# The value products of the last two token groups as seven block products on 2x2 blocks, with a new order of the whole kernel

## The chip, the cores and the metric

The kernel runs on one core of one Trainium2 chip. The time is the device time of one launch in microseconds (us); of several runs the median is taken. A core has five engines that work side by side, each through its own queue in order: PE (TensorE, matrix products, with results in the eight banks of PSUM), DVE (VectorE), ACT (ScalarE), POOL (GpSimd) and SP (SyncE, which here issues DMAs). In the profile PEld is the load of a matmul's weights, which overlaps PE.

## The reference

What is computed is an attention over 4 batches x 8 heads x 768 positions x 64, with three full causal heads and five that see only four first keys and a window of 64, and behind it a feed-forward block with a gate. The attention's output becomes x, 3072 tokens x 512:

```python
def _moe_ref(x, w_gate, w_val, w_out) -> np.ndarray:
    g = x @ w_gate
    silu = g * (1.0 / (1.0 + np.exp(-g)))
    val = x @ w_val
    return (silu * val @ w_out).astype(np.float32)
```

w_gate and w_val are 512 x 1536, w_out is 1536 x 512. Inputs and output are float32; the kernel multiplies in float16 and sums in float32.

## The kernel before

The 3072 tokens are 24 tiles of 128, in six groups (g = 0 to 5) of four tiles, 512 tokens. Attention makes one tile of x after another: transposed q and k, scores (sc), exponentials on ACT (ex), masks (mask), products with v (val), division by the sums (nm), and a transpose into xt, by PE for the first eight tiles and by DMA (xdma) behind them.

For each group and each of 12 blocks j of 128 columns of the 1536, the feed-forward block runs five tasks. gate (L755, matmul at L759) multiplies the four 128-row parts of w_gate with xt: four matmuls of 512 columns into one bank. tanh (L765) on ACT, stt1 (L769) on DVE: (tanh + 1) times the gate's bank, into the buffer sil. vals is the same function as gate with w_val, four matmuls of 512 columns into another bank. stt2 (L775) on DVE: 0.5 x sil x vals' bank, into h_sb in float16.

The product of h with w_out is already made in 2x2 blocks with seven block products (seventh, L860; out<g>.p1 to p7, each 12 matmuls of 256 columns), with weight sums ws (L412), sums of h called hs (hsum, L831, 768 columns of float16, on DVE or POOL), and gathers oe (L886 to L898, mostly on DVE). Group 5 ends with last_sevens. Stores are issued by SP and ACT.

Every piece of work is a task of a plan with dependencies, buffers that it takes, and the engines that may run it. Nothing is scheduled by the compiler: three strings, made beforehand by a planner, fix everything. ORDER has two characters for each task, its number in base 62 (numbers from 3700 up are warming matmuls), and gives the order in which all tasks are written out; each engine runs its own tasks in that order. WAYS has a digit for each task, the engine among the allowed ones. SLOTS has the buffer of each ring that a task takes: raw (11 buffers of 128x1024 f32), sil, sig, xt and others, and for "gv", "o" and "big" a bank of PSUM.

Read out in this way, the old order has, behind the last attention product val23.0, 19 gates, 22 vals and the rest of the out products on PE; 45 stt, 22 oe and 16 hs on DVE; and 7 hs on POOL.

Of the kernel before, what the change touches and what calls it, by code (L numbers as in the profile page):

```python
# [40 lines left out]
WAYS = (
    "000000000000000000000000000000000000000000000000000000000000222212202202222022110100101101110001"
    "212100001000000000000000210012022201011011000000000000001100222212001010000000000001000000000000"
    "001200002201000000000001000000001000000010000000000220120000000000010000002000000000000020000220"
    "000000100100000000200010000000000020000000000000000000000000210002120000000000100000210001001000"
    "002202020020000001001000000002000000000000000021002000000000000000010001000202220000000001000000"
    "000010010000010002212100000010010000000100000000000000000000000000000000000000000000000000000000"
    "000000000000000000000000000000000000000000001100001100000000000000000000000000000000000000000000"
    "000000000000000000000000000000000000000110000000000000000000000000000000000000000000000000000000"
    "000000000000000000010001100011000000000001000000000000000000000000000000000000000000000000000000"  # L50
    "000000001000000000000000000000110000000000000000000000000000000000000000000000000000000000000011"
    "010000110000000000010000000000000000000000000000000000000000000000000000000000000000101000000000"
    "00011001011000000"
)
SLOTS = (
    "001423105578362145403027124360570705626241030877537806901020040702261213013460614010320001264002"
    "430101642120400017524426503000204102434011162426123000254004600122630164212045422322214400101000"
    "130234502420041024003014523602204224610042412422404222212503602112240050221240143404020044225200"
    "005411611104105112030140001212061231013100700167007612020117123450061751067110011241201016300460"
    "216005211560201025311267261606003611020071110012121267117601100231114700730027201774112050100016"  # L60
    "610661265014600771040126102070067023342264511137001010641241015202110066116102500050001512722100"
    "4111232013411120253127611561005111201141005015610026745406"
)
DIGITS = "0123456789ABCDEFGHIJKLMNOPQRSTUVWXYZabcdefghijklmnopqrstuvwxyz"

# [54 lines left out]
def kernel(  # L120
# [13 lines left out]
    nc = tc.nc  # L134
# [11 lines left out]
    DFF = moe_w_gate.shape[1]  # L146
# [57 lines left out]
    def copy(task, dst, src):  # L204
        if task.way == "ACT":
            nc.scalar.copy(out=dst, in_=src)  # L206
        else:
            ENG[task.way].tensor_copy(out=dst, in_=src)  # L208
# [165 lines left out]
    T_w = {}  # L374
# [380 lines left out]
    def gate(g, j, c, wsb, d):  # L755
        xt = xts[g]
        ps = d[g, j, c] = buf("gv", [128, 512], FP, "gv")[:, 0:c[1] - c[0]]
        for kk in range(4):
            nc.tensor.matmul(  # L759
                ps, wsb[:, kk, j * 128:(j + 1) * 128], xt[:, kk, c[0]:c[1]],  # L760
                start=(kk == 0), stop=(kk == 3))

    def tanh(g, j, c):
        sg[g, j, c] = buf("sig", [128, 512], FP, "sig")[:, 0:c[1] - c[0]]
        nc.scalar.activation(out=sg[g, j, c], in_=gs[g, j, c], func=AF.Tanh, scale=0.5)  # L765

    def stt1(g, j, c):
        sl[g, j, c] = buf("sil", [128, 512], FP, "sil")[:, 0:c[1] - c[0]]
        nc.vector.scalar_tensor_tensor(  # L769
            out=sl[g, j, c], in0=sg.pop((g, j, c)), scalar=1.0, op0=ALU.add,  # L770
            in1=gs.pop((g, j, c)), op1=ALU.mult)
# [186 lines left out]
    def tasks_of_sevens(g, T_h):  # L958
# [66 lines left out]
        for x, parts in enumerate(([c11, c12], [c21, c22])):  # L1025
            st = T_st[g, x] = P.add(f"st{g}.h{x}", ["SP", "ACT"],
                                    (lambda x=x: store_half(g, x)), deps=parts)
            T_stored[g, x] = [P.lands(st)]

    for g in range(NG):  # L1030
        w = SIZES[g] * 128
        xs = [T_xe[t] for t in range(FIRST[g], FIRST[g + 1])]
        T_h = {}
        for j in range(NJ):
            parts = [(0, 256), (256, 512)] if g == 0 and j < HALVES else [(0, w)]
            for c in parts:
                a = P.add(f"gate{g}.{j}.{c[0]}", ["PE"],
                          (lambda g=g, j=j, c=c: gate(g, j, c, wg_sb, gs)),
                          deps=xs[c[0] // 128:c[1] // 128] + [T_w["g", j // 2][j % 2]],
                          takes=["gv"])  # L1040
                th = P.add(f"tanh{g}.{j}.{c[0]}", ["ACT"],
                           (lambda g=g, j=j, c=c: tanh(g, j, c)), deps=[a], takes=["sig"])
                s1 = P.add(f"stt1 {g}.{j}.{c[0]}", ["DVE"],
                           (lambda g=g, j=j, c=c: stt1(g, j, c)), deps=[th], takes=["sil"])
# [4 lines left out]
                was = [T_p[g - 2, p] for p in ((6, 7) if j < NK else (3, 4))] if g > 1 else []  # L1049
                was += T_hs[g - 2, 4] if g > 1 and j < NK else []  # L1050
# [3 lines left out]
                P.uses(a, "gv", s1)  # L1054
                P.uses(v_, "gv", s2)
                P.uses(th, "sig", s1)
                P.uses(s1, "sil", s2)
                P.uses(T_first_x[g], "xt", a, v_)
        if g < SEVENS:
            tasks_of_sevens(g, T_h)  # L1060
            continue
# [66 lines left out]
```

## Time and profile before

| | us |
|---|---|
| median of 3 runs (238.83 to 239.19) | 239.04 |
| the profiled execution | 239.03 |
| its span, first to last instruction | 237.2 |
| last matmul's work ends | 233.73 |

| engine | busy us | instructions |
|---|---|---|
| PE | 230.5 | 2211 |
| DVE | 194.5 | 362 |
| ACT | 141.2 | 217 |
| POOL | 110.6 | 132 |

Times in the profile's views count from the span's start. In a view by groups, a row has the line of the program, the engine, the operation, output and input with their shapes, the count, the busy time, the mean duration of one, and the idle time before them with what ended it. A recorded duration of one instruction is longer than the distance at which the next can follow it on the same engine, so distances are read from a timeline, and PE's from the chain of work. Matmuls are pipelined: their recorded durations overlap.

### The profile page before, as it was taken

The page shows a single profiled execution, that of the slowest core. Times are in us where ns is not written, and L with a number is a line of the kernel's source. Part 1 is how long each engine was busy: PE and PEld are TensorE (multiplying, and loading weights), DVE is VectorE, ACT ScalarE, POOL GpSimd, SP SyncE. Part 2 cuts the span into 40 slices and gives each one's busy share as a digit, 9 for nine tenths or more (in the row PEclk, how much of TensorE's full clock was granted, in tenths as well). Part 3 has the DMA queues.
Part 4 walks back from the last instruction along what each step waited for, and adds up shares of the span by engine and source line. Part 5 has one row for each costly group of instructions (what it writes and reads, how often), then busy time and mean ns, then how long its engine had stood idle before and what let it go on. Part 6 is the DMA issues. An engine that isn't in the chain of part 4 may idle for free.

```text
span 237.2 us, 5639 instructions
## 1 busy us (share of the span) xinstructions
PE 230.5 (97%) x2211; PEld 146.0 (62%) x2211; DVE 194.5 (82%) x362; ACT 141.2 (59%) x217; POOL 110.6 (47%) x132
## 2 busy tenths in 40 slices
PE   7899999999999999999999999999999999999994
PEld 2577865655457778655464557766555565557883
DVE  2689999998999699698968989786969867788873
ACT  3699999889599879839575485384242232231010
POOL 7386577937484940998600550884000000525500
PEclk9999999999999999999999999999999999999999
DMA  6999999999999999999798124011620000220044
GB/s 173 351 343 366 326 346 356 358 350 296 271 238 165 236 291 182 289 164 188 196 171 207 34 48 87 4 22 20 203 44 0 3 0 0 87 92 1 20 183 155
DMA packets 67194, 40.73 MB, mean 172 GB/s; under 512 B 25184, under 2 KB 61024, under 8 KB 67168
## 3 DMA queue, kind: packets, MB, share of 16 engines
q1 hardware_dynamic: 65248, 37.50, 63.4%
q10 hardware_dynamic: 1920, 2.88, 3.3%
q8 instruction: 17, 0.28, 0.5%
q14 instruction: 9, 0.07, 0.1%
HBM read 28.31 MB, written 6.29 MB: 146 GB/s over the span
## 4 chain that ended last, share of the span: by engine, by line
PE 92%; DVE 3%; DMA 2%; ACT 1%; issue 0%; DVEq 0%
PE banks L759 51%; PE banks L860 23%; PE banks L567 8%; PE banks L597 6%; PE banks L473 2%; DMA raw<-in_q_dram 2%; PE banks L621 1%; DVE wt_sb L412 1%; DVE sil L769 1%; ACT hq L206 0%; PE banks L321 0%; DVE kT L208 0%; DVE hq L212 0%; DVE qT L208 0%; DVE xb L605 0%; DVE h_sb L775 0%
## 5 line engine op out<-in xcount | busy, mean ns | idle before, releaser
L765 ACT ACTIVATE sig<-banks 128x512 f32<-128x512 f32 (+1 forms) x76 | 42.7, 574 | 54.6 <-PE banks L759 47.5
L759 PE MATMUL banks<-xt,wg_sb 128*128 128x512 f16 (+1 forms) x304 | 71.4, 368 | 0.5 <-DVE sil L769 0.5
L759 PE MATMUL banks<-xt,wv_sb 128*128 128x512 f16 (+1 forms) x304 | 70.9, 368 | 0.0
L579 ACT ACTIVATE e<-banks 128x1024 f16<-128x1024 f32 (+2 forms) x68 | 59.5, 910 | 15.0 <-PE banks L567 6.3
L769 DVE SCALAR_TENSOR_TENSOR sil<-sig,banks 128x512 f32<-128x512 f32 (+1 forms) x76 | 48.8, 655 | 14.3 <-ACT sig L765 13.6
L775 DVE SCALAR_TENSOR_TENSOR h_sb<-sil,banks 128x512 f16<-128x512 f32 (+1 forms) x76 | 48.9, 655 | 2.8 <-PE banks L759 1.8
L860 PEld LDWEIGHTS <-h_sb 128*128 128x128 f16 x420 | 40.4, 98 | 8.5
L759 PEld LDWEIGHTS <-wv_sb 128*128 128x128 f16 x304 | 28.6, 98 | 26.9
L759 PEld LDWEIGHTS <-wg_sb 128*128 128x128 f16 x304 | 28.1, 98 | 27.2 <-issue 0.8
L587 POOL TENSOR_TENSOR e<-e,m 128x640 f16<-128x640 f16 (+1 forms) x17 | 28.0, 1655 | 19.8 <-ACT e L579 19.4
L831 POOL TENSOR_TENSOR h_sb<-h_sb 128x768 f16<-128x768 f16 x13 | 21.2, 1640 | 22.5 <-DVE hs_sb L831 16.7
L898 DVE TENSOR_TENSOR out_sb<-banks,out_sb 128x512 f32<-128x512 f32 x37 | 25.1, 688 | 7.4 <-PE banks L860 7.0
L860 PE MATMUL banks<-wt_sb,h_sb 128*128 128x256 f16 x216 | 26.2, 273 | 0.0
L831 POOL TENSOR_TENSOR hs_sb<-h_sb 128x768 f16<-128x768 f16 x3 | 4.9, 1639 | 45.1 <-PE banks L860 41.2
L860 PE MATMUL banks<-wo_sb,h_sb 128*128 128x256 f16 x204 | 25.1, 273 | 0.0
L597 PEld LDWEIGHTS <-e 128*128 128x128 f16 x472 | 18.0, 97 | 5.8 <-DVE e L587 0.2
L567 PEld LDWEIGHTS <-kT 64*128 64x128 f16 x472 | 14.4, 94 | 9.3 <-issue 8.7
L567 PE MATMUL banks<-qT,kT 64*128 64x128 f16 x472 | 19.7, 218 | 0.2 <-ACT qT L206 0.2
L597 PE MATMUL banks<-vt,e 128*128 128x65 f16 x472 | 19.7, 193 | 0.1
L206 ACT CAST hq<-raw 128x1024 f16<-128x1024 f32 (+1 forms) x16 | 14.7, 936 | 5.2 <-DMA raw<-in_q_dram 3.2
L605 DVE TENSOR_TENSOR xb<-banks,rc 128x512 f16<-128x512 f32 x24 | 16.6, 692 | 0.8
L208 POOL CAST vt<-raw 64x512 f16<-64x512 f32 x23 | 14.0, 607 | 2.3 <-DMA raw<-in_v_dram 1.3
(64 smaller groups left out, 192.9 us busy)
## 6 DMA issues: line engine op xcount, KB each, us to landing
raw<-in_v_dram SPq DMA_DIRECT2D x12, 512.0 KB, 5.8
raw<-in_q_dram SPq DMA_DIRECT2D x8, 512.0 KB, 6.2
raw<-in_k_dram SPq DMA_DIRECT2D x8, 512.0 KB, 5.3
raw<-in_moe_w_gate_dram SPq DMA_DIRECT2D x6, 512.0 KB, 8.6
raw<-in_moe_w_val_dram SPq DMA_DIRECT2D x6, 512.0 KB, 8.2
raw<-in_moe_w_out_dram SPq DMA_DIRECT2D x6, 512.0 KB, 7.9
out_dram<-out_sb SPq DMA_DIRECT2D x6, 512.0 KB, 4.4
raw<-in_q_dram SPq DMA_DIRECT2D x8, 256.0 KB, 6.4
```

Source lines behind the costliest of these rows:

```text
L567: nc.tensor.matmul(sc[:, c:c + n, :], weights, moving, start=first, stop=last)
L579: nc.scalar.activation(out=to, in_=src, func=AF.Exp, scale=scale)
L587: ENG[task().way].tensor_tensor(out=ev, in0=ev, in1=mm, op=ALU.mult)
L597: nc.tensor.matmul(avs[t][:, odd, n * 66:n * 66 + 65], ee, vv, start=(m == 0), stop=(m == len(bl) - 1))
L605: nc.vector.tensor_tensor(out=xb.rearrange("p n o d -> p o n d"), in0=av[:, :, :, 0:64], in1=rc.to_broadcast([128, 2, 4, 64]), op=ALU.mult)
L759: nc.tensor.matmul(ps, wsb[:, kk, j * 128:(j + 1) * 128], xt[:, kk, c[0]:c[1]], start=(kk == 0), stop=(kk == 3))
L765: nc.scalar.activation(out=sg[g, j, c], in_=gs[g, j, c], func=AF.Tanh, scale=0.5)
L769: nc.vector.scalar_tensor_tensor(out=sl[g, j, c], in0=sg.pop((g, j, c)), scalar=1.0, op0=ALU.add, in1=gs.pop((g, j, c)), op1=ALU.mult)
L775: nc.vector.scalar_tensor_tensor(out=hs[g, j][:, c[0]:c[1]], in0=sl.pop((g, j, c)), scalar=0.5, op0=ALU.mult, in1=vs.pop((g, j, c)), op1=A ...
L831: ENG[T_hs[g, x][part].way].tensor_tensor(out=to, in0=a, in1=b, op=op)
L860: nc.tensor.matmul(rooms[g, p][:, x, lo:hi], left[:, j, 128 * x:128 * x + 128], right[:, j, lo:hi], start=(on is None and (j == 0 if apart ...
L898: nc.vector.tensor_tensor(out=cell(*to), in0=room, in1=plus, op=ALU.add)
```

## The change

The vals products of groups 4 and 5 (WINO) are replaced. The group's x is split into 2x2 blocks of 256 columns by token halves x and halves y of the 512 inputs; w_val into blocks of 256 rows by 768 columns. Seven block products take the place of eight. For each s = 0, 1, 2, the tasks wp<g>.<s>.<p> make two 128-column blocks of each half, j = 2s, 2s + 1 and 6 + 2s, 7 + 2s: seven products of four matmuls of 256 columns, where vals had 16 matmuls of 512.

New tasks beside them:

- vw (L412's pattern, function msum): eight differences of parts of w_val, 128x768 float16 in SBUF, made once for both groups, on DVE or POOL.
- xs (xsum): four sums of x blocks for each group, 128x512 float16 in SBUF, on DVE or POOL.
- wy (w_copy): five copies of a bank, 128x512 float32, for each s, on ACT or DVE. P1 is copied from bank X, P6 is then added to bank X by PE and copied, then P7, then P4, so the bank's four products form a chain over PE and the copying engine.
- wa (w_add, c11): a sum of two SBUF pieces, 128x512 float32, on POOL or DVE.
- wb (w_add, c22 and c12): a sum of a bank and an SBUF piece, on DVE.
- stt2 of these groups (stt2_w) reads its second operand from those SBUF pieces (in raw buffers), not from a bank.

The rest of the computation is as before, but ORDER, WAYS and SLOTS are new throughout. Read out, they give:

| | before | after |
|---|---|---|
| vals tasks | 76 | 52 |
| wp tasks | 0 | 42 |
| hs on DVE / POOL | 31 / 17 | 19 / 29 |
| wy on ACT / DVE | | 26 / 4 |
| wa on POOL / DVE | | 4 / 2 |
| wb on DVE | | 12 |
| vw on DVE / POOL | | 3 / 5 |
| xs on DVE / POOL | | 2 / 6 |
| warming tasks beside the first | 2 | 2 |

A stretch of the new order, PE's, DVE's and POOL's tasks, on each line a PE task and what is written between it and the next:

```
PE wp4.2.6    DVE stt2 4.1.0    POOL hs3.2.0
PE wp4.1.7    DVE stt1 4.6.0
PE gate4.7.0  DVE stt1 4.2.0
PE wp4.2.7    POOL hs3.2.1      DVE stt2 4.6.0
PE gate4.9.0  DVE stt1 4.7.0
PE gate4.8.0  DVE stt2 4.7.0
PE wp4.1.4    DVE stt1 4.3.0    POOL xs5.1
PE wp4.2.2    DVE wa4.1.c11
PE wp4.1.5
PE wp5.0.1    POOL xs5.2        DVE wb4.1.c22
PE out3.p6    DVE stt2 4.0.0    POOL wa4.2.c11   DVE oe3.c11
PE wp5.0.2    DVE stt1 4.9.0
PE wp4.1.3    POOL xs5.3        DVE stt2 4.3.0
PE gate5.0.0  DVE oe3.r6
PE wp4.2.4    POOL hs3.4.0      DVE stt2 4.2.0
```

The core of the diff, without the strings:

```diff
+    WINO = {"v": (4, 5), "g": ()}
...
+        ENG[T_mw[mat, i][kk].way].tensor_tensor(
+            out=m_sums[mat, i, kk], in0=a, in1=b, op=ALU.subtract)
...
+        a, b, op = {1: (A[1, 0], A[1, 1], ALU.add), 2: (Z[:, 0], A[0, 0], ALU.subtract),
+                    3: (A[0, 0], A[1, 0], ALU.subtract),
+                    4: (A[0, 1], Z[:, 1], ALU.subtract)}[i]
+        ENG[T_xs[g, i].way].tensor_tensor(out=Z[:, i - 1], in0=a, in1=b, op=op)
+
+    W_ON = {1: "X", 6: "X", 7: "X", 4: "X", 2: "Y", 5: "Z", 3: "Z"}
...
+        for m in range(2):
+            at = slice(128 * (2 * s + m), 128 * (2 * s + m) + 128)
+            for kk in range(2):
...
+                nc.tensor.matmul(
+                    w_rooms[on][:, m], right, left[:, kk],
+                    start=(begins and m == 0 and kk == 0), stop=(kk == 1),
+                    skip_group_check=True)
...
+    def w_copy(mat, g, s, name):
+        to = w_cell(mat, g, s, name)
+        copy(T_wc[mat, g, s, name], to, w_rooms[mat, g, s, "Y" if name == "y2" else "X"])
+
+    def w_add(mat, g, s, name):
+        to = w_cell(mat, g, s, name)
+        other = w_cell(mat, g, s, "y2") if name == "c11" else w_rooms[mat, g, s, "Z"]
+        ENG[T_wc[mat, g, s, name].way].tensor_tensor(out=to, in0=other, in1=to, op=ALU.add)
...
+    def stt2_w(g, j):
+        hs[g, j] = h_sb[:, g % 2, j]
+        nc.vector.scalar_tensor_tensor(
+            out=by_halves(hs[g, j]), in0=by_halves(sl.pop((g, j, (0, 512)))),
+            scalar=0.5, op0=ALU.mult, in1=w_cells("v", g, j), op1=ALU.mult)
...
+            p1 = product(1, xs + w_lo)
+            r1 = copied("r1", [p1])
+            p6 = product(6, [r1, T_xs[g, 2]] + T_mw[mat, 2])
+            u2 = copied("u2", [p6])
+            p7 = product(7, [u2, T_xs[g, 3]] + T_mw[mat, 3])
+            u3 = copied("u3", [p7])
+            p4 = product(4, [u3] + T_mw[mat, 4])
+            p2 = product(2, xs + w_lo)
+            y2 = copied("y2", [p2, r1])
...
+            c11 = added("c11", [y2])
+            c21 = copied("c21", [p4, c11])
...
+            p5 = product(5, [T_xs[g, 1]] + T_mw[mat, 1])
+            c22 = added("c22", [p5, u3])
+            p3 = product(3, [c22, T_xs[g, 4]] + w_hi)
+            c12 = added("c12", [p3])
```

More of the change, by code (lines that the diff above doesn't have):

```diff
@@ new lines @@
+    T_mw = {}
+    for mat in ("v", "g"):
+        for i in range(1, 5) if WINO[mat] else []:
+            T_mw[mat, i] = []
+            for kk in range(2):
+                before = T_mw[mat, i // 2][kk:kk + 1] if i in (2, 4) else []
+                T_mw[mat, i].append(P.add(
+                    f"vw{i}.{kk}" + mat, ["DVE", "POOL"],
+                    (lambda mat=mat, i=i, kk=kk: msum(mat, i, kk)),
+                    deps=[y for n in range(6) for y in T_w[mat, n]] + before,
+                    takes=(["hq"] if i == 4 else ["e"]) if mat == "g"
+                    else [] if kk else ["raw"],
+                    after=T_mw[mat, i][:1]))
@@ new lines, with sums_of_x @@
+    T_xs, T_wp, T_wc = {}, {}, {}
+    def sums_of_x(g, xs):
+        first = T_first_x[g]
+        for i in range(1, 5):
+            T_xs[g, i] = P.add(
+                f"xs{g}.{i}", ["DVE", "POOL"], (lambda i=i: xsum(g, i)),
+                deps=xs + {2: [T_xs.get((g, 1))], 4: [T_xs.get((g, 2))]}.get(i, []),
+                takes=[] if i > 1 else ["raw"], after=[T_xs[g, 1]] if i > 1 else [])
+            P.uses(first, "xt", T_xs[g, i])
+        sum1 = T_xs[g, 1]
+        P.uses(sum1, "raw", T_xs[g, 2], T_xs[g, 4])
@@ new lines, in tasks_of_wino, with product, copied, added @@
+    def tasks_of_wino(mat, g, xs):
+        first, sum1 = T_first_x[g], T_xs[g, 1]
+        for s in range(NK // 2):
+            w_lo, w_hi = list(T_w[mat, s]), list(T_w[mat, s + 3])
+            def product(p, deps, s=s):
+                t = T_wp[mat, g, s, p] = P.add(
+                    f"wp{g}.{s}.{p}" + mat, ["PE"], (lambda: w_product(mat, g, s, p)),
+                    deps=deps, takes=["gv"] if p in (1, 2, 5) else [])
+                if p in (1, 2, 4):
+                    P.uses(first, "xt", t)
+                else:
+                    P.uses(sum1, "raw", t)
+                if p >= 4:
+                    for y in T_mw[mat, {4: 4, 5: 1, 6: 2, 7: 3}[p]]:
+                        if y.takes:
+                            P.uses(y, y.takes[0], t)
+                return t
+            def copied(name, deps, s=s):
+                T_wc[mat, g, s, name] = P.add(
+                    f"wy{g}.{s}.{name}" + mat, ["ACT", "DVE"], (lambda: w_copy(mat, g, s, name)),
+                    deps=deps, takes=["raw"] if name in ("r1", "u2") else [])
+                return T_wc[mat, g, s, name]
+            def added(name, deps, s=s):
+                T_wc[mat, g, s, name] = P.add(
+                    f"w{'a' if name == 'c11' else 'b'}{g}.{s}.{name}" + mat,
+                    ["POOL", "DVE"] if name == "c11" else ["DVE"],
+                    (lambda: w_add(mat, g, s, name)), deps=deps)
+                return T_wc[mat, g, s, name]
+            p1 = product(1, xs + w_lo)
[7 more added lines that the diff above has]
+            y2 = copied("y2", [p2, r1])
+            P.uses(p2, "gv", y2)
+            c11 = added("c11", [y2])
+            c21 = copied("c21", [p4, c11])
+            P.uses(p1, "gv", c21)
+            p5 = product(5, [T_xs[g, 1]] + T_mw[mat, 1])
+            c22 = added("c22", [p5, u3])
+            p3 = product(3, [c22, T_xs[g, 4]] + w_hi)
+            c12 = added("c12", [p3])
+            P.uses(p5, "gv", c12)
@@ L1033 @@
         T_h = {}
+        if g in WINO_ALL:
+            sums_of_x(g, xs)
+        for mat in ("g", "v"):
+            if g in WINO[mat]:
+                tasks_of_wino(mat, g, xs)
         for j in range(NJ):
@@ L1036 @@
             for c in parts:
[L1037 to L1044, printed above, removed]
+                below = ("c11", "c21") if j < NK else ("c12", "c22")
@@ new lines @@
+                head = "r1" if j < NK else "u2"
+                if g in WINO["g"]:
+                    th = P.add(f"tanh{g}.{j}.{c[0]}", ["ACT"], (lambda g=g, j=j: tanh_w(g, j)),
+                               deps=[T_wc["g", g, j % NK // 2, y] for y in below], takes=["sig"])
+                    s1 = P.add(f"stt1 {g}.{j}.{c[0]}", ["DVE"], (lambda g=g, j=j: stt1_w(g, j)),
+                               deps=[th], takes=["sil"])
+                    P.uses(T_wc["g", g, j % NK // 2, head], "raw", s1)
+                else:
+                    a = P.add(f"gate{g}.{j}.{c[0]}", ["PE"],
+                              (lambda g=g, j=j, c=c: gate(g, j, c, wg_sb, gs)),
+                              deps=xs[c[0] // 128:c[1] // 128] + [T_w["g", j // 2][j % 2]],
+                              takes=["gv"])
+                    th = P.add(f"tanh{g}.{j}.{c[0]}", ["ACT"],
+                               (lambda g=g, j=j, c=c: tanh(g, j, c)), deps=[a], takes=["sig"])
+                    s1 = P.add(f"stt1 {g}.{j}.{c[0]}", ["DVE"],
+                               (lambda g=g, j=j, c=c: stt1(g, j, c)), deps=[th], takes=["sil"])
+                    P.uses(a, "gv", s1)
+                    P.uses(T_first_x[g], "xt", a)
@@ new lines @@
+                was = [T_p[g - 2, p] for p in ((6, 7) if j < NK else (3, 4))] if g > 1 else []
+                was += T_hs[g - 2, 4] if g > 1 and j < NK else []
+                P.uses(th, "sig", s1)
+                if g in WINO["v"]:
+                    cells = [T_wc["v", g, j % NK // 2, y] for y in below]
+                    s2 = P.add(f"stt2 {g}.{j}.{c[0]}", ["DVE"],
+                               (lambda g=g, j=j: stt2_w(g, j)), deps=[s1] + cells + was)
+                    T_h.setdefault(j, []).append(s2)
+                    P.uses(s1, "sil", s2)
+                    P.uses(T_wc["v", g, j % NK // 2, head], "raw", s2)
+                    continue
@@ L1053 @@
                 T_h.setdefault(j, []).append(s2)
[L1054 removed]
                 P.uses(v_, "gv", s2)
[L1056 removed]
                 P.uses(s1, "sil", s2)
[L1058 removed]
+                P.uses(T_first_x[g], "xt", v_)
         if g < SEVENS:
```

154 lines of the change are left out of this document (110 added, 44 removed).

## The prediction

> **What bounds the kernel now.** I read the page's busy shares and clock first, then what PE waited for, then a table by stage, then the chain of work that ended last.
>
> ```profile
> PE 230.5 (97%) x2211; PEld 146.0 (62%) x2211; DVE 194.5 (82%) x362; ACT 141.2 (59%) x217; POOL 110.6 (47%) x132
> ...
> PEclk9999999999999999999999999999999999999999
> ```
>
> ```profile
> PE banks L321 <- POOL ident L234: 1.4, 1, 1.4
> PE banks L473 <- DVE hq L212: 0.8, 1, 0.8
> PE banks L759 <- DVE sil L769: 0.5, 1, 0.5
> PE banks L567 <- ACT qT L206: 0.2, 1, 0.2
> ```
>
> ```profile
> core 0: us, PE busy (x) PEld busy (x) DVE busy (x) ACT busy (x) POOL busy (x), PEclk, DMA share, GB/s
> ...
> 170.81:220.62 49.81, 49.81 (x298) 29.01 (x297) 39.56 (x67) 13.29 (x23) 8.07 (x5) 1.00 0.09 30
> 220.62:237.20 16.58, 13.10 (x120) 11.49 (x118) 10.41 (x19) 0.96 (x2) 3.28 (x2) 1.00 0.36 128
> ```
>
> PE is busy 97% of the span at full clock, and over the whole run it waits 2.9 us for named engines. From the end of val23.0 (170.81) to the last gate or value product (220.62) it has no gap: 49.81 of 49.81. So matmul time taken out there is worth its full length, for as long as the other engines keep pace. In that stretch DVE is busy 39.56 of 49.81 us (79%), ACT 27%, POOL 16%. The stage is PE's, and DVE is the next engine in line.
>
> **What PE saves.** Two rows of the chain give the spacing of the two kinds of matmul.
>
> ```profile
> 175.57 5.18 PE banks L759 x24
> 180.75 1.31 PE banks L860 x12
> ```
>
> A 512-column matmul takes 5.18/24 = 0.216 us, a 256-column one 1.31/12 = 0.109. Removed: 2 groups x 12 blocks x 4 = 96 of the first, 20.7 us. Added: 2 groups x 3 values of s x 7 products x 4 = 168 of the second, 18.3 us. PE saves **2.4 us**. Without any new wait: 239.03 - 2.4 = 236.6 (239.03 is the profiled execution; its span is 237.2, and the median of the runs is 239.04, so sums on the one hold for the other).
>
> **What the other engines get.** Durations are in these groups, spacings in the two DVE timelines behind them.
>
> ```profile
> L775 DVE SCALAR_TENSOR_TENSOR h_sb<-sil,banks 128x512 f16<-128x512 f32 x68 | 45.7, 682 | 2.7 <-PE banks L759 1.8
> ...
> L765 ACT ACTIVATE sig<-banks 128x512 f32<-128x512 f32 x68 | 39.8, 596 | 54.6 <-PE banks L759 47.5 <-DVE sil L769 6.8
> ...
> L898 DVE TENSOR_TENSOR out_sb<-banks,out_sb 128x512 f32<-128x512 f32 x37 | 25.1, 688 | 7.4 <-PE banks L860 7.0
> ...
> L831 POOL TENSOR_TENSOR h_sb<-h_sb 128x768 f16<-128x768 f16 x13 | 21.2, 1640 | 22.5 <-DVE hs_sb L831 16.7 <-DVE h_sb L831 5.7
> ...
> L831 DVE TENSOR_TENSOR h_sb<-hs_sb,h_sb 128x768 f16<-128x768 f16 x11 | 6.0, 551 | 0.0
> ...
> L412 POOL TENSOR_TENSOR wt_sb<-wo_sb,wt_sb 128x512 f16<-128x512 f16 x4 | 4.6, 1158 | 6.6 <-DVE wt_sb L412 6.5
> ...
> L206 ACT COPY out_sb<-banks 128x512 f32<-128x512 f32 x3 | 1.7, 582 | 0.0
> ```
>
> ```profile
> 195.78 0.68 DVE L769 SCALAR_TENSOR_TENSOR sil<-sig,banks 128x512 f32<-128x512 f32 x1
> 196.38 0.68 DVE L898 TENSOR_TENSOR out_sb<-banks,out_sb 128x512 f32<-128x512 f32 x1
> ...
> 212.98 0.55 DVE L831 TENSOR_TENSOR h_sb<-hs_sb,h_sb 128x768 f16<-128x768 f16 x1
> 213.45 0.68 DVE L769 SCALAR_TENSOR_TENSOR sil<-sig,banks 128x512 f32<-128x512 f32 x1
> ```
>
> Back to back, a 512-wide f32 instruction costs DVE 0.60 us and a 768-wide f16 sum 0.47. The 30 copies out of banks go 26 to ACT (0.58 each, 15.1 us in a stage where ACT has over 36 us free: hidden) and 4 to DVE. DVE also gets 12 sums wb and two wa (0.60 each), two x sums and three weight differences. Against that, 12 more hs sums move to POOL. In the new order DVE has, from val23.0 to the last stt2: 48 stt (28.8 us), 12 wb (7.2), 9 oe (5.4), two wa (1.2), three wy (1.8), and about 3.1 of nm23, sums and differences: **47.5 us**. PE has there 9 out products of 12 (11.8), 23 gates of 4 x 0.216 (19.9), 37 wp of 4 x 0.109 (16.2) and val23.0 (0.4), 48.2 us, and the last tanh, stt1 and stt2 add about 2.1: 50.3. So DVE goes from 79% to 94%. It still fits, with **2.8 us** to spare, if nothing holds it.
>
> The PSUM chain p1, copy, p6, copy, p7, copy, p4 is covered: the order puts other products between its members. The tightest place is p7 to p3 of group 4, s 0: two gates (1.73 us) against a copy and a sum (0.58 + 0.69). The first p7 also needs vw2.1, xs4.4 and vw3.1 in turn on POOL (1.64 + 1.16 + 1.64), started when val23.1 is due; that ends about 0.5 us after p7's turn. I count this at nothing in the sum, since it overlaps the lateness below, and at up to 1.4 in the range. The new raw buffers come when the loads are over. At the start the order changes little (two fills of the same lengths, the same first products): nothing, plus or minus 0.5 (PE's waits there are 2.4 in all, above). No DMA is added; the stores stay eight on ACT and eight on SP. Behind the last gate stand twelve out products instead of ten. The first that needs a late h, out5.p7, waits for stt2 5.10.0, hs5.1.1 (0.47) and hs5.3.1 on POOL (1.64), with oe4.r6 and r67 ahead in DVE's queue, and comes six products (7.9 us) after the last gate: covered while DVE is on time, and passed on in full once it is late.
>
> **The new hold.** This decides it. stt2 before reads one SBUF operand (sil) and banks. The new stt2 of groups 4 and 5 reads sil and the cells, both in SBUF, and so does wa. Before has no f32 instruction of that kind on DVE; it has f16 ones, and one of them met POOL:
>
> ```profile
> 59.43 1.04 POOL L208 CAST hq<-raw 128x1024 f16<-128x1024 f32 x1 [1.46 <-DMA raw<-in_q_dram]
> ```
>
> ```profile
> 59.53 1.54 DVE L412 TENSOR_TENSOR wt_sb<-wo_sb 128x512 f16<-128x512 f16 x2
> 61.00 0.68 DVE L769 SCALAR_TENSOR_TENSOR sil<-sig,banks 128x512 f32<-128x512 f32 x1
> ```
>
> ```profile
> L412 DVE TENSOR_TENSOR wt_sb<-wo_sb x3: 411/414/1212, 59.5 to 62.8; 128x512 f16<-128x512 f16 x3
> ```
>
> Of three alike, one took 1212 ns against 411 and 414: it started at 59.53 under a POOL cast (59.43 to 60.47) and ended 0.27 us after it. It stood still until POOL was nearly done. With one operand in PSUM there is no such hold:
>
> ```profile
> 204.24 3.24 POOL L831 TENSOR_TENSOR hs_sb<-h_sb 128x768 f16<-128x768 f16 x2 [41.25 <-PE banks L860]
> ```
>
> ```profile
> 204.80 1.28 DVE L775 SCALAR_TENSOR_TENSOR h_sb<-sil,banks 128x512 f16<-128x512 f32 x2
> ```
>
> Two stt2 ran under two POOL sums at 1.28 for both, as elsewhere. [...]
>
> The old order keeps its f16 two-SBUF sums out of POOL's spans. The new order doesn't do so for the new instructions: by the positions of the tasks between PE's, with POOL at 1.64 (768-wide) and 1.16 (512-wide), 9 of the 24 new stt2 start inside a POOL instruction by the latest reading, 20 by the earliest. And POOL's share of the stage rises from 8.07 us in five to about 34 (13 hs, 5 xs, 2 vw, 4 wa).
>
> I walked DVE's order by hand from wp4.2.6, each instruction at 0.60, an stt2 waiting for the POOL instruction under way and the next POOL instruction for it. In us from that point: stt2 4.1.0 0.0 to 0.6, POOL hs3.2.0 0.6 to 2.2, stt1 4.6.0 and 4.2.0 to 1.8, stt2 4.6.0 held to 2.2 and done 2.8, POOL hs3.2.1 2.8 to 4.5, stt1 4.7.0, stt2 4.7.0 held to 4.5; and so on. To stt2 4.10.0, 28 instructions (16.8 us) meet 8 holds (4.6 us); in the rest 8 holds come to 7.2. Together 16 holds, 11.8 us, 0.74 each. As the held row ended 0.27 after POOL where alone it lasts 0.41, I take 0.14 off each: 9.6. Less DVE's 2.8 to spare: **6.8 us late**, and PE waits for it, because gates, p3 and p6 wait for banks, sums and copies that stand behind the held stt2 in DVE's queue.
>
> Bounds of this unknown: nothing, if two f32 operands are not held or DVE always comes first; at the other end 11.8 + 1.4 = 13.2, every hold in full, nothing spare and the first p7 late. The nearest row is the held L412, so I take the hold.
>
> **Sum:** 239.03 - 2.4 + 6.8 = 243.4; say **243.5**.
>
> **Rivals.**
>
> *The hold doesn't come (not slower).* The mechanism: at stt2 of groups 4 and 5, an f32 SCALAR_TENSOR_TENSOR with both operands in SBUF runs beside POOL at 0.60, or gets through first. For it: the only held row is f16, of another operation, and one event. Against it: the same two SBUF operands. Price: DVE at 94% keeps pace, PE loses only the 0.5 at the first p7: 236.6 + 0.5 = 237.1, with 236.3 to 238. It decides where holds sum to under 2.8 (to spare) + 2.4 (PE's gain) = 5.2 us, 0.33 per hold at 16.
>
> *DVE is too full even so.* DVE idled 7.6 us for ACT's tanh in the old stage by the row below; at 94% there is room for 2.8. If half of that idling stays (3.8), it is 1 us late, plus 0.5 to 1.4 at the first p7: 236.6 + 1.0 + 1.0 = 238.6, between 238 and 239.5.
>
> ```profile
> L769 DVE SCALAR_TENSOR_TENSOR sil<-sig,banks 128x512 f32<-128x512 f32 x22 | 14.9, 684 | 7.6 <-ACT sig L765 7.5
> ```
>
> [...]
>
> **How the numbers follow.** Held: 0.60, from 240 to 246.5, point 243.5. Not held: 0.28, 236.3 to 238. Too full: 0.12, 238 to 239.5, of which half lies within 0.2% (0.48 us, about what a measurement of this kernel can tell from no change), a third faster, the rest slower. That gives faster 0.32, same 0.06, slower 0.62. The range takes most of both signs: 236.5 to 246.5; the likeliest case's own is 240 to 246.5.
>
> **What would show it.** Right: the group of stt2 reading sil and raw has a mean over 1.0 us with a minimum near 0.68, its long ones under POOL spans; PE has several us of waits after 171, on DVE; POOL instructions themselves stretch here and there. PE's 256-column products stay at 0.109. Wrong: that group's mean is 0.69, PE's waits stay under 1 us in all, and the end comes 2 us earlier. Wrong on PE's side: 168 matmuls that don't hold 0.109 because their weights change each time, though L860's do the same.

## The result, and the profile after

| | before | after |
|---|---|---|
| median of the runs | 239.0 us (238.83 to 239.19) | 253.23 us (251.71 to 254.62, 4 runs) |
| ratio to before | | 1.0594, 95% interval 1.0511 to 1.0677 |
| profiled execution: time, span | 239.03, 237.2 us | 251.71, 249.9 us |

The change makes the kernel 14.2 us slower. The direction and the mechanism are the predicted ones. The size is not: 4.5 us were forecast, and the result lies above the range. One thing is needed to compare profiles: the first product of group 4 starts at 161.59 us in this one, but up to 3.0 us later in some of those below, mostly because PE waited for DMAs and for ACT (1.5 and 1.0 us in the run with the reduce in group 4 alone, the latest), ahead of all that the edits touch; so beside the medians some stretches are given from that product to the end of the profile.

The page of the changed kernel, busy shares and granted clock:

```profile
PE 231.6 (93%) x2283; PEld 153.4 (61%) x2283; DVE 214.8 (86%) x358; ACT 157.6 (63%) x256; POOL 159.3 (64%) x161
...
PEclk9999999999999999999999999999999899999999
...
L1148 DVE SCALAR_TENSOR_TENSOR h_sb<-sil,raw 128x512 f16<-128x512 f32 x24 | 27.2, 1144 | 0.2
```

PE fell from 97% to 93% of a longer span. DVE is 20.3 us busier (194.5 before) with four instructions fewer. 5.4 of that is the new mix of work: the run whose POOL only writes (below) has the same 358 instructions on DVE and 199.9 us. The other 14.9 are instructions that became longer; the last row is a group of them (busy us, mean ns, idle us before it), taken up below. What PE waited for, late in the kernel (total us, times, longest):

```profile
PE banks L762 <- DVE sil L772: 3.7, 3, 2.5
PE banks L1104 <- DVE raw L1125: 3.4, 2, 2.1
PE banks L1104 <- DVE raw L1084: 1.4, 1, 1.4
```

All three name DVE. Before, the largest wait for DVE anywhere was 0.8. The stage in five slices (busy us and count of PE, PEld, DVE, ACT, POOL, then granted clock, DMA share, GB/s):

```profile
180.00:190.00 10.00, 9.22 (x66) 6.23 (x65) 9.76 (x13) 4.80 (x10) 9.29 (x7) 1.00 0.04 15
190.00:200.00 10.00, 7.92 (x50) 5.33 (x49) 8.17 (x13) 3.67 (x8) 4.34 (x3) 0.83 0.00 0
200.00:210.00 10.00, 8.55 (x62) 5.84 (x61) 9.96 (x14) 2.68 (x6) 5.28 (x3) 1.00 0.01 2
210.00:220.00 10.00, 8.48 (x59) 5.52 (x57) 9.83 (x13) 5.53 (x12) 5.36 (x3) 1.00 0.28 105
220.00:230.00 10.00, 7.46 (x56) 5.21 (x54) 10.00 (x11) 4.25 (x8) 8.97 (x5) 1.00 0.01 2
```

Where PE had no gap before, it now idles 0.8 to 2.5 us of every ten, while DVE is all but full in four of the five. The group that the prediction named, the new stt2 of groups 4 and 5 (minimum, median, maximum ns):

```profile
L1148 DVE SCALAR_TENSOR_TENSOR h_sb<-sil,raw x24: 674/1006/2124, 178.8 to 233.5; 128x512 f16<-128x512 f32 x24
```

The shortest takes 674 ns; the mean is 1144, by the group's row above. DVE's timeline shows which are long, and POOL's shows why (start, duration, us):

```profile
166.17 1.61 DVE L590 TENSOR_TENSOR e<-e,m 128x640 f16<-128x640 f16 x1
167.71 3.42 DVE L1054 TENSOR_TENSOR raw<-wv_sb,raw 128x768 f16<-128x768 f16 x2
...
188.01 1.67 DVE L1148 SCALAR_TENSOR_TENSOR h_sb<-sil,raw 128x512 f16<-128x512 f32 x1
189.61 0.68 DVE L901 TENSOR_TENSOR out_sb<-banks,out_sb 128x512 f32<-128x512 f32 x1
190.21 1.52 DVE L1148 SCALAR_TENSOR_TENSOR h_sb<-sil,raw 128x512 f16<-128x512 f32 x1
...
194.85 0.68 DVE L1148 SCALAR_TENSOR_TENSOR h_sb<-sil,raw 128x512 f16<-128x512 f32 x1
```

```profile
167.40 1.40 POOL L1084 TENSOR_TENSOR raw<-xt,raw 128x512 f16<-128x512 f16 x1
168.76 1.95 POOL L1054 TENSOR_TENSOR raw<-wv_sb 128x768 f16<-128x768 f16 x1
...
187.99 1.15 POOL L1084 TENSOR_TENSOR raw<-xt 128x512 f16<-128x512 f16 x1
189.09 4.14 POOL L834 TENSOR_TENSOR h_sb<-h_sb 128x768 f16<-128x768 f16 x2
193.19 1.16 POOL L1084 TENSOR_TENSOR raw<-xt,raw 128x512 f16<-128x512 f16 x1
```

The stt2 at 188.01 starts 0.02 us after a POOL sum of 1.15 and takes 1.67. The one at 190.21 starts inside the first of two POOL sums and takes 1.52; those two sums take 4.14 together instead of 3.24. Between them the L901 at 189.61, which reads a bank and one SBUF operand, takes its usual 0.68 under the same POOL sum, and the stt2 at 194.85, with POOL idle, takes 0.68. There are holds that the prediction did not count, too: the mask at 166.17 (1.61) and the two weight differences at 167.71 (3.42 for two). In the run whose POOL only writes (below), in the same order, the mask takes 0.48 and the two differences 1.02.

### The profile page after: what moved, and what is told of

It is laid out like the page before. It is cut to its first block, busy times and chain, and to the rows that moved or that the text cites. A ratio compares the mean times of both kernels' runs of the same rounds, so it can differ in the third digit from the quotient of the medians.

```text
span 249.9 us, 5873 instructions
## 1 busy us (share of the span) xinstructions
PE 231.6 (93%) x2283; PEld 153.4 (61%) x2283; DVE 214.8 (86%) x358; ACT 157.6 (63%) x256; POOL 159.3 (64%) x161
## 5 line engine op out<-in xcount | busy, mean ns | idle before, releaser
L762 PE MATMUL banks<-xt,wg_sb 128*128 128x512 f16 (+1 forms) x304 | 73.2, 371 | 4.5 <-DVE sil L772 3.7
L582 ACT ACTIVATE e<-banks 128x1024 f16<-128x1024 f32 (+2 forms) x68 | 59.3, 909 | 12.8 <-PE banks L570 9.8
L762 PE MATMUL banks<-xt,wv_sb 128*128 128x512 f16 (+1 forms) x208 | 47.6, 363 | 0.0
L834 POOL TENSOR_TENSOR h_sb<-h_sb 128x768 f16<-128x768 f16 x18 | 32.2, 1793 | 19.3 <-DVE hs_sb L834 17.4
L590 POOL TENSOR_TENSOR e<-e,m 128x640 f16<-128x640 f16 (+1 forms) x18 | 30.2, 1681 | 11.7 <-ACT e L582 11.3
L778 DVE SCALAR_TENSOR_TENSOR h_sb<-sil,banks 128x512 f16<-128x512 f32 (+1 forms) x52 | 32.7, 642 | 3.6 <-PE banks L762 2.5
L762 PEld LDWEIGHTS <-wv_sb 128*128 128x128 f16 x208 | 19.2, 98 | 17.7
L209 ACT COPY raw<-banks 128x512 f32<-128x512 f32 x27 | 15.2, 590 | 20.5 <-PE banks L1104 9.5
L901 DVE TENSOR_TENSOR out_sb<-banks,out_sb 128x512 f32<-128x512 f32 x37 | 24.8, 684 | 3.5 <-PE banks L863 2.9
L1148 DVE SCALAR_TENSOR_TENSOR h_sb<-sil,raw 128x512 f16<-128x512 f32 x24 | 27.2, 1144 | 0.2
L834 POOL TENSOR_TENSOR h_sb<-hs_sb,h_sb 128x768 f16<-128x768 f16 x6 | 11.5, 1918 | 4.6 <-DVE h_sb L834 4.6
```

What stands on the lines that cost most here:

```text
L582: nc.scalar.activation(out=to, in_=src, func=AF.Exp, scale=scale)
L590: ENG[task().way].tensor_tensor(out=ev, in0=ev, in1=mm, op=ALU.mult)
L762: nc.tensor.matmul(ps, wsb[:, kk, j * 128:(j + 1) * 128], xt[:, kk, c[0]:c[1]], start=(kk == 0), stop=(kk == 3))
L778: nc.vector.scalar_tensor_tensor(out=hs[g, j][:, c[0]:c[1]], in0=sl.pop((g, j, c)), scalar=0.5, op0=ALU.mult, in1=vs.pop((g, j, c)), op1=A ...
L834: ENG[T_hs[g, x][part].way].tensor_tensor(out=to, in0=a, in1=b, op=op)
L901: nc.vector.tensor_tensor(out=cell(*to), in0=room, in1=plus, op=ALU.add)
```

## The experiments

**One operand instead of two.** All 24 new stt2 lose their second SBUF operand. The order, the engines and the instruction's length stay.

```diff
-        nc.vector.scalar_tensor_tensor(
-            out=by_halves(hs[g, j]), in0=by_halves(sl.pop((g, j, (0, 512)))),
-            scalar=0.5, op0=ALU.mult, in1=w_cells("v", g, j), op1=ALU.mult)
+        nc.vector.tensor_reduce(
+            out=by_halves(hs[g, j]), in_=w_cells("v", g, j).unsqueeze(3),
+            axis=mybir.AxisListType.X, op=ALU.max)
```

> The changed kernel with the 24 value instructions of groups 4 and 5 (stt2) replaced by a DVE reduction of the same 128x512 size that reads the cells alone, so the product with sil is left out; same order, same engines, same count. Hold theory: DVE instructions with two SBUF operands stand still under POOL's sums, so with one operand these 24 take 0.68 to 0.70 us each instead of 1.14, POOL's late sums go back to 1.64, and the time falls from 253.2 by the 11 us that they were held and about 2 us of what POOL was held: 239 to 242. Fullness theory: DVE simply has too much work behind group 3; its work is the same here, so 251 to 254.

Measured: 238.89 us, ratio to before 0.9998 (0.997 to 1.0027). That is just under the 239 to 242 of the hold theory. The group, and slices of the stage:

```profile
L1148 DVE TENSOR_REDUCE h_sb<-raw x24: 670/679/686, 178.6 to 220.6; 128x512 f16<-128x512 f32 x24
```

```profile
170.00:180.00 10.00, 8.57 (x61) 5.63 (x60) 8.64 (x16) 4.62 (x8) 5.41 (x4) 1.00 0.25 72
180.00:190.00 10.00, 10.00 (x76) 7.20 (x74) 10.00 (x17) 6.05 (x12) 9.62 (x8) 1.00 0.03 9
190.00:200.00 10.00, 10.00 (x79) 7.64 (x78) 9.68 (x17) 3.53 (x7) 3.73 (x4) 1.00 0.01 2
200.00:210.00 10.00, 10.00 (x69) 6.57 (x68) 9.50 (x17) 6.22 (x12) 7.05 (x5) 1.00 0.28 105
210.00:220.00 10.00, 10.00 (x79) 7.43 (x77) 9.95 (x17) 5.30 (x10) 7.76 (x5) 1.00 0.01 2
```

No instruction of the 24 is held, and from 180 on PE has no gap, with the same instructions on POOL. The second SBUF operand of these 24 is worth 253.23 - 238.89 = 14.3 us by the medians: more than the whole loss. In the profiles, from the first product of group 4 to the end, it is 12.9 (88.3 us in the changed kernel, 75.4 here). The slices show something else, needed below: even without holds DVE has only 0.9 us free in the forty from 180 on, and 1.4 in the ten before.

**POOL writes but does not read.** The stt2 keep both operands, and POOL's late sums become memsets.

```diff
+    def add_up(task, late, out, in0, in1, op):
+        if late and task.way == "POOL":
+            for _ in range(2):
+                nc.gpsimd.memset(out, 0.0)
+            return
+        ENG[task.way].tensor_tensor(out=out, in0=in0, in1=in1, op=op)
...
-        ENG[T_hs[g, x][part].way].tensor_tensor(out=to, in0=a, in1=b, op=op)
+        add_up(T_hs[g, x][part], g >= 3, to, a, b, op)
```

The calls in vw, xs and wa are replaced in the same way.

> The changed kernel with POOL's late sums (hs of groups 3 to 5, weight differences, x sums, wa) replaced by two memsets of the same output each, so POOL reads nothing there and these sums are left out of the result; DVE's work is untouched, with both SBUF operands. Hold theory, if what is held is the reading: stt2 at 0.68 to 0.70 us, time 237 to 240. If POOL holds DVE by writing too: stt2 still near 1.0 us, 246 to 252. Fullness theory: 251 to 254.

Measured: 236.24 us, ratio 0.9898 (0.9851 to 0.9944), just under the 237 to 240 of the hold theory.

```profile
L1154 DVE SCALAR_TENSOR_TENSOR h_sb<-sil,raw x24: 681/685/693, 176.3 to 218.3; 128x512 f16<-128x512 f32 x24
```

The same two-operand instruction is not held by a POOL that only writes, and PE's timeline has no gap from 160 us to its end. 236.2 is close to the 236.6 that the prediction's first sum gave without any new wait: PE's saving is real, and DVE with all its new work keeps pace. (POOL's work is a little lighter here, 147.0 us in all against 154.0 in the first experiment.)

**The late sums on DVE.** Nothing is left out; POOL gets no late sum.

```diff
+        for t in self.tasks:
+            late = t.name[:2] in ("vw", "xs", "wa") or t.name[:3] in ("hs3", "hs4", "hs5")
+            if late and t.way == "POOL":
+                t.way = "DVE"
```

> The changed kernel with the late sums of POOL (hs of groups 3 to 5, weight differences, x sums, wa) moved to DVE at the same places of the order; nothing is left out. Hold theory: stt2 at 0.68 to 0.70 us, but DVE gets about 11 us more work in a stretch that had 2.8 to spare, so about 8 us late: 243 to 248, faster than 253.2 in spite of the added work. Fullness theory: 11 us more work on the engine that bounds: 262 to 266.

Measured: 247.92 us, ratio 1.0363 (1.0339 to 1.0387), at the upper end of the hold theory's 243 to 248.

```profile
180.00:200.00 20.00, 17.51 (x129) 12.43 (x128) 19.62 (x35) 9.12 (x17) 0.00 (x0) 1.00 0.01 4
```

With POOL at rest in the stage the 24 stt2 are not held (a mean of 688 ns), but now DVE is full with work. Taking all late sums off POOL, in this order, is no way out.

**The hold by itself.** Behind the kernel before stand six stages, each of eight DVE instructions, five of them beside a row of POOL instructions; a single execution.

```diff
+    stages = [(lambda: two(fb[:, 0:512]), None, 0),
+              (lambda: two(fb[:, 0:512]), pool_sum, 4),
+              (lambda: two(bank), pool_sum, 4),
+              (lambda: two(fb[:, 0:512]), lambda: nc.gpsimd.memset(pool_out, 0.0), 8),
+              (lambda: two(fb[:, 0:512]),
+               lambda: nc.gpsimd.tensor_copy(out=pool_out, in_=pool_in[0]), 6),
+              (lambda: nc.vector.tensor_reduce(out=half, in_=fa[:, 0:512].unsqueeze(2),
+                                               axis=mybir.AxisListType.X, op=ALU.max),
+               pool_sum, 4)]
```

> The kernel before, and behind its end six stages of eight DVE instructions (128x512 f32 in, f16 out) beside POOL work: both operands in SBUF alone; both in SBUF beside sums 128x768 f16 on POOL; one in SBUF and one in a bank beside these sums; both in SBUF beside memsets; both in SBUF beside copies; a reduction with one SBUF operand beside sums. Hold theory: 0.69 us each in stages 1, 3, 6; in stages 2 and 5 some DVE instructions of 1 to 2.2 us and POOL sums over 1.64; stage 4 at 0.69 if only reading holds. Intrinsic theory (the instruction is slow with two SBUF operands whatever POOL does): 1.1 us in stages 1, 2, 4 and 5 alike.

The stages on DVE (two SBUF operands alone, then beside sums; one operand in a bank beside sums; two beside memsets; two beside POOL copies; a reduce beside sums), and POOL's part in the second and third:

```profile
240.60 5.77 DVE L1114 SCALAR_TENSOR_TENSOR raw<-raw 128x512 f16<-128x512 f32 x8
...
246.67 1.58 DVE L1111 COPY raw<-raw 128x4 f32<-128x4 f32 x1 [0.29 <-POOL raw L1110]
248.16 9.70 DVE L1114 SCALAR_TENSOR_TENSOR raw<-raw 128x512 f16<-128x512 f32 x8
...
259.66 5.73 DVE L1114 SCALAR_TENSOR_TENSOR raw<-raw,banks 128x512 f16<-128x512 f32 x8
...
265.69 0.67 DVE L1111 COPY raw<-raw 128x4 f32<-128x4 f32 x1 [0.30 <-POOL raw L1110]
265.77 5.77 DVE L1114 SCALAR_TENSOR_TENSOR raw<-raw 128x512 f16<-128x512 f32 x8
...
272.74 8.27 DVE L1114 SCALAR_TENSOR_TENSOR raw<-raw 128x512 f16<-128x512 f32 x8
...
282.80 5.72 DVE L1126 TENSOR_REDUCE raw<-raw 128x512 f16<-128x512 f32 x8
```

```profile
246.59 7.82 POOL L1118 TENSOR_TENSOR raw<-raw 128x768 f16<-128x768 f16 x4
...
258.09 6.77 POOL L1118 TENSOR_TENSOR raw<-raw 128x768 f16<-128x768 f16 x4
```

Two of the six rows of eight are longer than the 5.77 alone: 9.70 beside POOL sums, 8.27 beside POOL copies. The hold goes both ways with the sums, since POOL's four take 7.82 there against 6.77 beside the operand in a bank. One operand in a bank, a reduce, or a POOL that only writes: no hold of the eight (5.73, 5.72, 5.77). So of these rows the held ones are those with two SBUF inputs on DVE beside a POOL that reads.

**Half the dose.** The reduce only in group 4:

```diff
+        if g == 4:
+            nc.vector.tensor_reduce(
+                out=by_halves(hs[g, j]), in_=w_cells("v", g, j).unsqueeze(3),
+                axis=mybir.AxisListType.X, op=ALU.max)
+            return
```

> As the first experiment, but only in group 4: its 12 stt2 become a reduce of the cells alone (silu times value left out there), those of group 5 keep their two SBUF operands. Theory (each hold passes on in full): about half of the 14.3 us remains, 244 to 248, and the 12 of group 5 keep a mean over 1.0 us. Rival (one group's holds are what matters, for instance those before the clock's fall at 180 to 200): within 1 us of 238.9 or of 253.2.

Measured: 248.19 us, ratio 1.0376 (1.0358 to 1.0395), just above the 244 to 248 of the hold theory. The groups (busy us, mean ns):

```profile
L1153 DVE SCALAR_TENSOR_TENSOR h_sb<-sil,raw 128x512 f16<-128x512 f32 x12 | 13.8, 1169 | 0.0
...
L1149 DVE TENSOR_REDUCE h_sb<-raw 128x512 f16<-128x512 f32 x12 | 8.1, 678 | 0.0
```

By the medians half the stt2 still cost 248.19 - 238.89 = 9.3 of the 14.3 us. But 3.1 us of the profiled execution were lost ahead of the stage: the first product of group 4 starts at 164.55 here, and at 161.44 with the reduce in both groups. From there to the end it takes 81.0 us against 75.4: 5.6 more, for 12 x (1.169 - 0.68) = 5.9 us of holds. The rival falls: half the holds cost about half of the 12.9.

**The same time without a hold.** The reduce in both groups, walking twice over its cells (the edit as against the first experiment):

```diff
-            out=by_halves(hs[g, j]), in_=w_cells("v", g, j).unsqueeze(3),
+            out=by_halves(hs[g, j]), in_=w_cells("v", g, j).unsqueeze(3).to_broadcast([128, 2, 256, 2]),
```

> The 24 stt2 of groups 4 and 5 become the one-operand reduce of the first experiment, but each walks over its 512 cells twice, so that it is about 0.53 us longer (1.21 instead of 0.68) with nothing held; silu times value is left out. Theory 'DVE's lost time is all that counts': 24 x 0.53 = 12.7 us more on DVE, less at most 2.8 to spare, give 249 to 252 (238.9 + 9.9 to 12.7). Rival 'a hold costs more than its time, since POOL is stretched and comes late too': time lost on DVE alone is partly soaked up, 244 to 248, well under the 253.2 of the changed kernel with 11 us of holds.

Measured: 252.26 us, ratio 1.0531 (1.0487 to 1.0574), just above the upper end of the first theory and far from the rival's.

```profile
L1148 DVE TENSOR_REDUCE h_sb<-raw x24: 1203/1214/1220, 181.0 to 233.8; 128x512 f16<-128x1024 f32 x24
```

24 x (1.213 - 0.679) = 12.8 us more on DVE make the kernel 252.26 - 238.89 = 13.4 us longer by the medians. Here too some of it lies ahead: the first product of group 4 starts at 163.81, 2.4 us late. From there to the end it takes 86.6 us, 11.2 more than the 75.4, inside the first theory's 9.9 to 12.7. So most of the time lost on DVE is passed on, less little more than the 0.9 that DVE has free behind 180. In the changed kernel the same stretch is 12.9 us longer for 24 x (1.144 - 0.68) = 11.1 us of holds. There the holds cost somewhat more than their own time, so that part of the rival's claim is not refuted.

**An order that avoids the holds, and one that doesn't know them.** Same arithmetic, nothing left out. From the first product of group 4 on (161.6 us), the tasks get a new order, new buffers and a new choice of engine for sums and copies. Both orders come from the same search over the plan's tasks and dependences, each task with its duration from the profiles; only one search knew the hold. The edit is data alone, the tail of the three tables; two pairs of lines of the first order's:

```diff
-    "7hDVD5Ea7k8A8GD68HDW8B7i7uDhD8Eb8DDCDi7v8N8EDQ8C7w8YDj8I8ZDkD78JDR838T8W7y8QDl8FDz8XEe7lE08K8L8U"
+    "7hDVD5Ea7k8A8GD68HDW8B7i7uDhD8Eb8DDCDi7v8N8EDQ8C7w8YDj8I8ZDkD78JDR838T8W7y8QDl8FDz8XEe7lE08K8R8L"
...
-    "000000000000000000000000000000000000000000011111100110000000000010111100000000100000001000000000"
+    "000000000000000000000000000000000000000000000010100110000000000000100000000000000000000000000000"
```

> Same arithmetic as the changed kernel, nothing left out. From the first product of group 4 (161.6 us) on, the tasks stand in another order, with other buffers and another share of the sums between DVE and POOL (12 hs sums on POOL there instead of 16, and fewer vw and xs), found by a search over orders in which a DVE instruction with two SBUF operands and a POOL instruction that reads SBUF exclude each other, with durations from rows of the profiles. Hold theory: the holds fall from some 25 us (both engines together) to under 8 and lie where nobody waits; estimate 236 to 239. Rival (seven products for the values are too much for DVE or for PE's banks in any order): 242 or more.

> As the run before it (nothing left out, the same search, the same time, the same durations), but the search knows of no hold. Without holds it would end where the run before it does. Hold theory: it pays 19 us of holds (both engines together), estimate 244 to 248, and its stt2 of groups 4 and 5 have a mean near 1 us. Rival (the changed kernel's order was merely a poor one, and any good one does): 236 to 239.

Measured: 239.4 us for the first, ratio 1.0033 (1.0006 to 1.0061), just above its 236 to 239, and 249.53 for the second, ratio 1.0428 (1.0408 to 1.0447), above its 244 to 248. One row of each:

```profile
L1148 DVE SCALAR_TENSOR_TENSOR h_sb<-sil,raw 128x512 f16<-128x512 f32 x24 | 15.8, 687 | 0.1
```

```profile
L1148 DVE SCALAR_TENSOR_TENSOR h_sb<-sil,raw 128x512 f16<-128x512 f32 x24 | 24.4, 1032 | 0.1
```

The same 24 instructions take 687 ns in the mean or 1032, by the order, the buffers and the engines that the search chose (POOL has 150 instructions in the first and 158 in the second). The order that knows the hold is 10.1 us faster than the one that doesn't; from the first product of group 4 to the end of the profiles it is 8.4 (75.3 against 83.7). In the faster one PE still waited twice early in the stage:

```profile
169.46 1.81 PE L1104 MATMUL banks<-raw 128*128 128x256 f16 x15 [0.63 <-DVE raw L1054]
174.21 1.02 PE L762 MATMUL banks<-xt,wg_sb 128*128 128x512 f16 x4 [0.79 <-DVE out_sb L901]
```

**Three more orders.** The search with mended first steps, twice, and once with every task kept on the engine that the changed kernel gives it.

> Nothing left out. The search of the order free of holds once more, with its first steps mended by that run's profile (POOL is free at 161.6, not 160.1; a wa takes 1.26) and with every duration lengthened at random by up to 5% while it searches. In the run before, PE still waited 0.63 and 0.79 us after 165. Hold theory: 236.3 to 238.5, under the kernel before. Rival (what the search gains is used up by the scatter of real durations): 239 to 241, as before or slower.

> Nothing left out. Another result of the same mended search, from another seed, with 13 of the 24 hs sums on POOL instead of 11. Hold theory: the same as its sister, 236.3 to 238.5. Rival: 239 to 241; if the two differ by over 1 us, the single order matters more than the rule by which it was found.

> Nothing left out. Every task stays on the engine on which the changed kernel has it (16 hs sums, 5 xs, 3 vw and 4 wa on POOL), so each engine has the same instructions; only their order from 161.6 us on and the buffers are new, found by the same search with the holds. Theory 'the order decides, not the load': 236.5 to 239.5, and the stt2 of groups 4 and 5 have a mean under 0.85 us. Rival 'POOL's load itself is too much and sums must go back to DVE': 242 or more.

Measured, in this order: 242.1 us, ratio 1.0144 (1.0103 to 1.0185); 237.26, ratio 0.9931 (0.9905 to 0.9957); and 248.57, ratio 1.0392 (1.0368 to 1.0415). The second, page, group and slices:

```profile
PE 228.3 (97%) x2283; PEld 152.8 (65%) x2283; DVE 202.1 (86%) x364; ACT 158.5 (67%) x258; POOL 142.5 (61%) x153
```

```profile
L1148 DVE SCALAR_TENSOR_TENSOR h_sb<-sil,raw x24: 673/680/757, 179.4 to 221.1; 128x512 f16<-128x512 f32 x24
```

```profile
180.00:190.00 10.00, 10.00 (x68) 6.46 (x67) 9.86 (x19) 4.34 (x8) 2.80 (x2) 1.00 0.00 1
190.00:200.00 10.00, 10.00 (x78) 7.44 (x77) 10.00 (x18) 7.38 (x14) 2.82 (x2) 1.00 0.15 54
200.00:210.00 10.00, 10.00 (x76) 7.24 (x75) 9.74 (x17) 5.23 (x10) 4.06 (x3) 1.00 0.14 52
210.00:220.00 10.00, 10.00 (x78) 7.43 (x77) 9.62 (x17) 3.72 (x7) 7.04 (x5) 1.00 0.01 2
```

This kernel beats both: 1.9 us under the kernel before (239.15 in the same set of runs) and 16.0 under the changed one. PE has no gap in these forty us. DVE has 0.8 us free in them, and POOL works 16.7 us instead of the changed kernel's 24.3. But a good order is easily lost. Its sister, from the same search, came out at 242.1, above its theory's 238.5 and above the rival's 241: its stt2 have a mean of 880 ns, and PE waits for DVE three times for 1.0 us or more (1.3, 1.1, 1.0). The two differ by 4.8 us, so, as the expectation had it, the single order matters more than the rule by which it was found. The order with the engines kept missed by 9 us, with the mean at 1179:

```profile
L1148 DVE SCALAR_TENSOR_TENSOR h_sb<-sil,raw 128x512 f16<-128x512 f32 x24 | 27.4, 1179 | 0.1
```

So 'the order decides, not the load' is not shown. Whether POOL's load rules out any good order, or only this one was too tight, one run does not tell.

## Why the prediction was right and wrong

- **What bounds the kernel: right.** PE had no time to give away in the stage, and DVE coming late there made the kernel longer.
- **PE saves 2.4 us: right.** Without POOL's reads the kernel took 236.24, 2.8 under the 239.0 before. That run leaves sums out; it shows what this plan would give without holds. The rival *DVE too full even so* (238.6) fell with it: DVE kept pace with all its new work.
- **The new stt2 at the old one's length: right.** The forecast counts both at 0.60 us from one to the next. In the run whose POOL only writes, the stt2 with two SBUF operands had a median of 685 ns, against a mean of 682 for the old stt2 that read a bank.
- **The new hold: right as a mechanism.** The f32 stt2 with two SBUF operands took 1.67 and 1.52 us beside POOL's sums at 188.01 and 190.21, and 0.68 at 194.85 with POOL idle, and the rival *hold doesn't come* fell. "Mean over 1.0 us with a minimum near 0.68" came as 1144 and 674. Without the second operand the loss is gone (238.89 us); without POOL's reads too (236.24); with two of the orders that were made to keep them apart too (239.4 and 237.26).
- **The holds' own size: nearly.** Forecast 9.6 us in 16 holds, measured 11.1 in the 14 of the 24 that were held. The walk behind the 9.6 also let the next POOL instruction wait for an stt2; the held row of the kernel before shows nothing of that, with its POOL cast at the usual 1.04 us. What a run showed later is POOL's four sums at 7.82 us beside eight DVE instructions with two SBUF inputs, against 6.77.
- **The step that failed is "Less DVE's 2.8 to spare: 6.8 us late".** The spare was counted over the whole stretch from val23.0 on, as an average of 94%. Most of it lies ahead of the first stt2 (178.8 us). From 180 to 220 DVE is 98% full even where nothing is held (0.9 us free in the first experiment), and 12.8 us of longer instructions cost 11.2. In the changed kernel not even that came off: DVE is idle 2.3 us from 180 to 230, 1.8 of them between 190 and 200, where it waits for PE (1.1) and ACT (0.6). So 2.8 were taken off where 1.4 should have been added.
- **What was put at nothing was not.** The f16 instructions on DVE were given no hold, and the late first p7 (0.5) was not counted in the sum. The mask and the two differences lost 1.1 and 2.4 us. They are there with the reduce as well, where the time is 238.89 - 236.24 = 2.65 us above the run without POOL's reads; PE's waits there are 1.4 for L1084, an x sum behind them in DVE's queue, and 0.6 for the mask. And POOL, said to stretch "here and there", takes a median of 2020 ns for its six sums out of hs_sb and h_sb, 1644 with the reduce.
- **The range** ended at 246.5, though the text itself had bounds up to 13.2 for the holds, which is 249.8. Even that end is passed.

The forecast of 243.5 is 8.2 us under the profiled execution (251.71). The holds made DVE 11.3 us busier than with the reduce (214.8 against 203.5) where 9.6 were forecast: 1.7. The spare that was taken off, and the idle time that came on top: 2.8 + 1.4 = 4.2. What was put at nothing: 2.5 (75.4 us with the reduce against 72.9 without POOL's reads, from the first product of group 4 to the end). PE's saving was 0.4 larger. That makes 8.0 of the 8.2. Why DVE had to wait between 190 and 200 is argued below and not shown. The median, 253.23, is 1.5 above the profiled execution: it lies between two executions near 251.8 and two near 254.6, and of the latter there is no profile.

## What to carry to other kernels

Before an operand moves from a bank into SBUF, count the SBUF inputs of the DVE instruction that reads it: here eight with two of them took 9.70 us beside POOL's sums and 8.27 beside its copies, against 5.77 alone, four of the sums took 7.82 against 6.77, and an order made without the hold paid for it: 249.5, against 237.3 to 242.1 for three orders made with it. Planning for it alone is not enough: a fourth order made in that way, with every task kept on its engine, took 248.6. A spare counts only where the loss falls: read an engine's free time in slices behind the first new instruction, not over the whole stage. And before giving a change up, give its plan the hold that it ran into: the best of the four orders is 1.9 us faster than the kernel before, though the other three are not, and the kernel before was given no new order.

## What the runs showed of the hardware that was not expected

- A hold reads as a longer instruction, not as a wait: the row at 188.01 is 1.67 busy, the idle time before the group is 0.2 us in all, and DVE's busy share rises with it. The spread of one form (674 to 2124) gives it away.
- A small DVE copy with one SBUF source is held as well: 4 elements per partition took 1.58 us at the head of a POOL sum, and 0.17 with POOL idle. Unlike the stt2, it was longer beside a POOL that only writes, too: 0.67 at the head of the memsets.
- PE's granted clock fell to 0.83 in the slice 190 to 200, behind a wait of 2.1 us for a wb. Four matmuls of a gate took 1.91 us there, and 1.03 four us later:

```profile
194.00 1.91 PE L762 MATMUL banks<-xt,wg_sb 128*128 128x512 f16 x4
...
198.42 1.03 PE L762 MATMUL banks<-xt,wg_sb 128*128 128x512 f16 x4
```

DVE idles most in that slice, so the slow matmuls may be what it waited for. But the longest wait of the same profile, 2.5 us before 228.24, left the clock at 1.00, and the execution of 254.57 had a mean clock of 1.00 where the one of 251.71 had 0.993. So these runs don't show what makes the clock fall, or what its fall costs the kernel.
